# Four of the seven w2 blocks as the moving operand, three as stationary ones, and c and x loaded on the weights' queue, in a one-token transformer block

## The chip, the cores and the metric

The kernel runs on one core of a Trainium2 chip. Times are device microseconds (us) of one execution; where several executions are quoted, it is their median. The profile is one execution taken by the hardware profiler; its span (first to last instruction) is about 1.8 us shorter than the time of the same execution. The runs were made in several sets, each with its own executions of the kernel before ("the same rounds") and not all on one chip: the medians of the kernel before in these sets lie between 427.35 and 427.75 us, so a difference of some 0.2 us is safe only within a set. A ratio of two kernels is the mean time of one's fast runs over the mean of the other's fast runs of the same rounds, so it is not quite the ratio of the medians quoted beside it. The brackets after it are a 95% interval.

## The reference, cut to what matters

Two tokens (one for each of two batch entries) go through one conditioned transformer block. Attention reads a cache of 2 x 4 heads x 32768 x 128 for keys and as much for values, in bf16, 134 MB in all. Then comes an MLP whose second weight, w2, has 3584 x 1024 elements:

```python
mod = (_silu(c) @ w_mod).reshape(c.shape[0], 6, 1, -1)      # c: (2, 1024), w_mod: (1024, 6144)
sa, ca, ga, sb, cb, gb = ...                                # the six slices of mod
h = _layernorm(x) * (1 + ca) + sa
x = x + ga * attention(h, k_cache, v_cache, wq, wo)
h = _layernorm(x) * (1 + cb) + sb
x = x + gb * (gelu(_layernorm(h) @ w1 + b1) @ w2 + b2)      # w2: (3584, 1024)
```

With two tokens, each weight element is used twice. The kernel is a way of reading 178 MB.

## The kernel before: the parts that matter here

All large loads (weights, keys, values, weights) go through one queue, issued by SyncE ("SP") into a ring of buffers. c and x, 4 KB each, are issued by ScalarE ("ACT") at the start:

```python
T.dma("act", lambda e: e.dma_start(c16[:, :], c.rearrange("b (k p) -> (b k) p", p=128)), ...)
T.dma("act", lambda e: e.dma_start(x16[:, :], A_x.rearrange("b o (k p) -> (b o k) p", p=128)), ...)
...   # transposes of c and x, silu, layernorm; then wmod block by block
```

w2 comes in seven blocks q of 512 rows: three loads of two blocks (2 MB each), then block 6 in two pieces, 768 KB (j = 0, 1, 2) and 256 KB (j = 3). There are two ways to multiply a block with gT, the activations (128 rows, 2 useful columns):

- w2 as the *moving* operand: gT is the weight in the array, w2 streams through, 512 columns an instruction. The result is a row in `psS[0]`, spread over four groups of 32 partitions. It has to be copied to SBUF and turned into columns by fp32 matmuls (`to_columns`) before the rest can use it.
- w2 as the *stationary* operand: 128 x 128 pieces of w2 are loaded into the array and only 2 columns of gT move. The result is in columns (`psO`) at once.

```python
for q in range(6):                                   # blocks 0 to 5: w2 moves
    it = need("w2", q // 2)                          # queues the load if it is not yet; what reads it waits
    for j in range(4):
        for hf in range(2):
            t = 2 * (j % 2) + hf
            pe(... matmul(psS[0][32*t:32*t+32, :], lhsT=gT[:, 4*q+j, :], rhs=w[:, q % 2, j*DM+hf*512:j*DM+(hf+1)*512], ...))
load_row("dve", psS[0], "psS0", 3)                   # copy of the row to SBUF
for j in range(4):                                   # block 6: w2 is stationary
    it = need("w2", 3 if j < 3 else 4)
    if j == 3:
        to_columns(psO, "psO", 3, False, False)      # fp32 transposes of the row, added into psO
    for k in range(KT8):
        pe(... matmul(psO[:, 2*k:2*k+2], lhsT=w[:, lo:lo+128], rhs=gT[:, 24+j, 0:2], ...))
dve(mT = psO * mod(5)); dve(res_bf = mT + x1b)
pe(matmul(psM[0:16, 0:128], lhsT=res_bf, rhs=ident)); dve(res16 = psM)   # then the store
```

(The last two lines are in shorthand. `to_columns` has four fp32 matmuls; the profile records each of them twice, so they stand as x8 below.)

## Time and profile before

| | before |
|---|---|
| time, median of 4 runs | 427.35 us (427.31 to 427.46) |
| span of the profiled run | 425.5 us |
| load queue, share of the 16 DMA engines' span | 98.3% |
| third pair of w2 blocks / 768 KB piece / 256 KB piece landed at | 417.73 / 419.57 / 420.21 us |
| first vector step behind w2 (mT) | 422.59 us |

The first fence holds lines of the page of the kernel before: busy time by engine, the slices of the DMA engines (each digit a fortieth of the span, 9 meaning 90% or more) with what they moved, the load queue's line (packets, MB, share of the 16 engines' span), and the chain of waits by engine.

```profile
PE 301.5 (71%) x5116; PEld 236.0 (55%) x5116; DVE 166.9 (39%) x347; ACT 156.8 (37%) x269; POOL 4.9 (1%) x23
...
DMA  8999999999999999999999999999999999999992
GB/s 325 426 430 424 430 436 424 434 424 434 428 436 427 436 427 434 428 436 427 435 428 434 426 436 427 436 427 435 427 434 427 434 429 434 427 430 422 425 429 113
...
q1 hardware_dynamic: 14286, 178.28, 98.3%
...
DMA 79%; PE 18%; ACT 1%; SPq 1%; issue 0%; DVE 0%; DVEq 0%
```

The DMA engines are full from the second slice to the last but one. Most other work fits under them. A change can then pay only before the first byte or behind the last ones. So the tail is what to read. The next fence is the timeline of the kernel before from the second pair of w2 blocks on (start, duration, engine, source line, operation, shapes, and in brackets the engine's idle time and what ended it). L708 are the moving matmuls, L650 is the row copy, L654 are the transposes of the row, L719 the stationary matmuls, L722 is mT.

```profile
412.07 0.63 PE L708 MATMUL psS<-w,gT 128*32 128x512 bf16 x1
...
412.88 1.90 PE L708 MATMUL psS<-w,gT 128*32 128x512 bf16 x16 [0.18 <-DMA w<-in_B_w_dram]
...
417.77 1.90 PE L708 MATMUL psS<-w,gT 128*32 128x512 bf16 x16 [2.99 <-DMA w<-in_B_w_dram]
...
419.62 0.80 PE L719 MATMUL psO<-gT,w 128*128 128x2 bf16 x24
419.72 0.69 DVE L650 COPY S_sb<-psS 128x512 f32<-128x512 f32 x1 [9.06 <-PE psS L708]
...
420.47 1.87 PE L654 MATMUL psO<-half,S_sb 128*128 128x4 f32 x8
...
422.20 0.35 PE L719 MATMUL psO<-gT,w 128*128 128x2 bf16 x8
422.59 0.17 DVE L722 TENSOR_TENSOR mT<-psO,modT 128x16 f32<-128x16 f32 x1 [2.17 <-PE psO L719]
```

The third fence is the end of the chain of waits of the kernel before, followed back from the last instruction (start, us, what).

```profile
387.77 29.96 DMA w<-in_B_w_dram
...
417.77 1.93 PE psS L708 x15
...
419.72 0.70 DVE S_sb L650
...
420.47 1.87 PE psO L654 x8
422.34 0.23 PE psO L719 x8
...
422.59 0.19 DVE mT L722
```

After 414.78 (412.88 + 1.90) PE has nothing to do for 3 us. Then the load lands, and the row copy (0.70) and the transposes (1.87) come behind the last moving matmuls. All loads are in at 420.21, yet mT starts at 422.59, 2.38 us later.

The start, before: x is used at 7.08, the first wmod matmul runs at 10.25, and from the third block on PE waits for the load.

```profile
7.08 0.19 PE L403 MATMUL psM<-ident,x 16*128 16x16 bf16 x1 [2.16 <-DMA x<-in_A_x_dram]
...
10.25 1.04 PE L451 MATMUL psS<-wmod,inT 128*32 128x512 bf16 x8
...
14.85 0.61 PE L451 MATMUL psS<-wmod,inT 128*32 128x512 bf16 x8 [1.85 <-DMA wmod<-in_w_mod_dram]
```

### The profile page before, as it was taken

The numbers are of one execution on the slowest core, as the hardware profiler recorded it, in microseconds if no ns is written. First come the engines' busy times: TensorE is split into PE (matmuls) and PEld (weight loads), VectorE is DVE, ScalarE is ACT, GpSimd is POOL, SyncE is SP. The second block draws the span as 40 slices with busy tenths as digits, with TensorE's granted clock in tenths as the row PEclk, the third lists the DMA queues.
The fourth block names the chain that finished last, engine by engine and source line by source line (L and its number), as shares of the span: only waits on it lengthen the run. The fifth ranks groups of instructions, "written<-read, shape, count | busy, mean of one in ns | idle before, by whom it ended". The sixth has DMA issues, their size and how long they took to land.

```text
span 425.5 us, 11554 instructions
## 1 busy us (share of the span) xinstructions
PE 301.5 (71%) x5116; PEld 236.0 (55%) x5116; DVE 166.9 (39%) x347; ACT 156.8 (37%) x269; POOL 4.9 (1%) x23
## 2 busy tenths in 40 slices
PE   1446478778999789687778958796886773554674
PEld 1105158765877678577567838685774761113243
DVE  1102036544585375256435614662473351101211
ACT  2000026447457348244634724382355335000010
POOL 3000000000000000000000000000000000000000
PEclk9755569968899889698988978898898695655575
DMA  8999999999999999999999999999999999999992
GB/s 325 426 430 424 430 436 424 434 424 434 428 436 427 436 427 434 428 436 427 435 428 434 426 436 427 436 427 435 427 434 427 434 429 434 427 430 422 425 429 113
DMA packets 14367, 178.50 MB, mean 419 GB/s; under 512 B 1543, under 2 KB 1550, under 8 KB 2830
## 3 DMA queue, kind: packets, MB, share of 16 engines
q1 hardware_dynamic: 14286, 178.28, 98.3%
q8 instruction: 9, 0.15, 0.1%
q14 instruction: 8, 0.07, 0.0%
q10 hardware_dynamic: 64, 0.01, 0.0%
HBM read 178.28 MB, written 0.00 MB: 419 GB/s over the span
## 4 chain that ended last, share of the span: by engine, by line
DMA 79%; PE 18%; ACT 1%; SPq 1%; issue 0%; DVE 0%; DVEq 0%
DMA K<-in_A_k_cache_dram 59%; PE psKT L500 11%; DMA wo<-in_A_wo_dram 8%; DMA w<-in_B_w_dram 7%; DMA wmod<-in_w_mod_dram 5%; PE psS L512 3%; PE psO L542 1%; SPq L377 1%; ACT KT_sb L504 1%; PE psS L708 0%; PE psS L641 0%; PE psO L654 0%; ACT E_sb L533 0%; DVE S_sb L650 0%; PE psM L523 0%
## 5 line engine op out<-in xcount | busy, mean ns | idle before, releaser
L500 PE MATMUL psKT<-ident,K 128*128 128x128 bf16 x2048 | 173.4, 236 | 36.8 <-DMA K<-in_A_k_cache_dram 34.4
L500 PEld LDWEIGHTS psKT<-ident,K 128*128 128x128 bf16 x2048 | 132.6, 106 | 48.7 <-DMA K<-in_A_k_cache_dram 42.0
L506 DVE COPY KT_sb<-psKT 128x1024 bf16<-128x1024 bf16 x160 | 108.4, 689 | 116.1 <-PE psKT L500 115.8
L504 ACT ACTIVATE KT_sb<-psKT 128x1024 bf16<-128x1024 bf16 x96 | 98.0, 1021 | 130.5 <-PE psKT L500 130.2
L512 PE MATMUL psS<-qcur,KT_sb 128*128 128x8 bf16 x2048 | 88.3, 168 | 8.3 <-ACT KT_sb L504 7.2
L512 PEld LDWEIGHTS psS<-qcur,KT_sb 128*128 128x128 bf16 x2048 | 79.4, 99 | 13.8 <-ACT KT_sb L504 8.7
L542 PE MATMUL psO<-V,E_sb 128*32 128x512 bf16 x512 | 39.0, 435 | 5.3 <-DMA V<-in_A_v_cache_dram 4.6
L533 ACT ACTIVATE E_sb<-S_sb,negm 128x256 bf16<-128x256 f32 x64 | 32.3, 505 | 9.5 <-DVE negm L529 8.6
L517 DVE TENSOR_REDUCE m1c<-S_sb 128x8 f32<-128x512 f32 x32 | 21.9, 686 | 14.3 <-ACT S_sb L516 13.3
L516 ACT ACTIVATE S_sb<-psS 128x512 f32<-128x512 f32 x32 | 19.0, 592 | 13.9 <-PE psS L512 13.9
L542 PEld LDWEIGHTS psO<-V,E_sb 128*32 128x32 bf16 x512 | 12.0, 104 | 17.5 <-DMA V<-in_A_v_cache_dram 5.6
L451 PE MATMUL psS<-wmod,inT 128*32 128x512 bf16 x64 | 8.0, 593 | 13.4 <-DMA wmod<-in_w_mod_dram 13.4
L641 PE MATMUL psS<-wo,atT 128*32 128x512 bf16 x64 | 7.6, 627 | 12.0 <-DMA wo<-in_A_wo_dram 12.0
L422 ACT ACTIVATE stat<-stat 128x2 f32<-128x2 f32 x3 | 0.6, 203 | 38.4 <-DVE stat L421 38.4
L472 PE MATMUL psS<-wq,inT 128*32 128x512 bf16 x64 | 7.5, 627 | 7.0 <-DMA wq<-in_A_wq_dram 6.0
L533 ACT ACTIVATION_READ_ACCUMULATOR E_sb<-S_sb,negm 128x1 f32 x64 | 12.2, 190 | 0.0
L451 PEld LDWEIGHTS psS<-wmod,inT 128*32 128x32 bf16 x64 | 1.2, 108 | 19.0 <-DMA wmod<-in_w_mod_dram 18.8
L641 PEld LDWEIGHTS psS<-wo,atT 128*32 128x32 bf16 x64 | 1.8, 128 | 16.7 <-DMA wo<-in_A_wo_dram 14.6
L650 DVE COPY S_sb<-psS 128x512 f32<-128x512 f32 x2 | 1.4, 692 | 22.1 <-PE psS L641 13.0
L563 PE MATMUL psM<-msum,hmat 128*128 128x128 f32 x16 | 4.2, 346 | 7.5 <-DVE msum L557 7.5
L457 ACT ACTIVATE S_sb<-psS 128x512 f32<-128x512 f32 x1 | 0.6, 597 | 23.7 <-DVE S_sb L459 23.7
L459 DVE COPY S_sb<-psS 128x512 f32<-128x512 f32 x1 | 0.7, 692 | 21.5 <-PE psS L451 21.5
(115 smaller groups left out, 135.6 us busy)
## 6 DMA issues: line engine op xcount, KB each, us to landing
K<-in_A_k_cache_dram SPq DMA_DIRECT2D x32, 2048.0 KB, 31.7
V<-in_A_v_cache_dram SPq DMA_DIRECT2D x32, 2048.0 KB, 35.0
wmod<-in_w_mod_dram SPq DMA_DIRECT2D x8, 1536.0 KB, 17.8
wq<-in_A_wq_dram SPq DMA_DIRECT2D x4, 2048.0 KB, 37.5
wo<-in_A_wo_dram SPq DMA_DIRECT2D x4, 2048.0 KB, 29.0
w<-in_B_w_dram SPq DMA_DIRECT2D x4, 1792.0 KB, 39.3
w<-in_B_w_dram SPq DMA_DIRECT2D x3, 2048.0 KB, 31.0
w<-in_B_w_dram SPq DMA_DIRECT2D x1, 768.0 KB, 27.8
```

The lines of the kernel that those rows point to most:

```text
L377: T.dma("sp", lambda e, dst=dst, src=cur.src: e.dma_start(dst, src), key=cur.sem, writes=[cur.reg], frees=old)
L451: pe(lambda e, w=it.view, k=k, ch=ch, n=n, q=q: e.matmul(bank[n][32 * q:32 * q + 32, :], lhsT=inT[:, k, :], rhs=w[:, ch * 512:(ch + 1) * 512],
L472: pe(lambda e, w=it.view, k=k, ch=ch, n=n, q=q: e.matmul(bank[n][32 * q:32 * q + 32, :], lhsT=inT[:, k, :], rhs=w[:, k % 2, ch * 512:(ch + ...
L500: pe(lambda e, kq=kq, jj=jj, w=it.view, t=t: e.transpose(psKT[kq][:, jj * 128:(jj + 1) * 128], w[:, t, :], ident[:, :]), reads=[it.reg, "i ...
L504: act(lambda e, src=src: e.activation(KT_sb[g8][:, :, :], src, ACT.Copy), reads=[f"psKT{kq}"], writes=[f"KT_sb{g8}"], sem=f"ev{cc}_{g8}")
L506: dve(lambda e, src=src: e.tensor_copy(KT_sb[g8][:, :, :], src), reads=[f"psKT{kq}"], writes=[f"KT_sb{g8}"], sem=f"ev{cc}_{g8}")
L512: pe(lambda e, t=t, jj=jj: e.matmul(ps[:, t * HPG:(t + 1) * HPG], lhsT=KT_sb[g8][:, jj, :], rhs=qcur[:, :], start=True, stop=True), reads= ...
L516: act(lambda e: e.activation(Sc, ps[:, :].rearrange("p (t h) -> p h t", h=HPG), ACT.Copy), reads=[preg], writes=[f"S_sb{i % 2}_{cc}"], sem ...
L517: dve(lambda e: e.tensor_reduce(m1c[:, :, cc], Sc, AX.X, ALU.max), reads=[f"S_sb{i % 2}_{cc}"], writes=[f"m1c{cc}"])
L533: act(lambda e: e.activation(E_sb[:, :, h, :], S_sb[j][:, h, :].rearrange("p (u t) -> p u t", t=4), ACT.Exp, bias=negm[:, h:h + 1], scale= ...
L542: pe(lambda e, t4=t4, tg=tg, q=q: e.matmul(psO[32 * q:32 * q + 32, :], lhsT=E_sb[:, tg // 4, :, :].rearrange("p h t -> p (h t)"), rhs=it.v ...
L641: pe(lambda e, w=it.view, g=g, j=j, hf=hf, q=q: e.matmul(psS[0][32 * q:32 * q + 32, :], lhsT=atT[g][:, j, :], rhs=w[:, j, hf * 512:(hf + 1 ...
```

## The change

Two edits in one. First, c and x are issued by SyncE behind the first wmod block, on the queue of the weights. Second, only blocks 0 to 3 of w2 stay moving. The row copy and the transposes follow them at once, and blocks 4, 5 and 6 are stationary. The intent is to do the row's detour while PE waits for the third pair, so that only short work stands behind the last landings.

```diff
-    T.dma("act", ... c16 ...)
-    T.dma("act", ... x16 ...)
+    need("wmod", 0)
+    T.dma("sp", ... c16 ...)
+    T.dma("sp", ... x16 ...)
...
-    for q in range(6):
+    for q in range(4):
         it = need("w2", q // 2)
         ...                                    # moving matmuls, as before
     load_row("dve", psS[0], "psS0", 3)
-    for j in range(4):
-        it = need("w2", 3 if j < 3 else 4)
-        if j == 3:
-            to_columns(psO, "psO", 3, False, False)
-        for k in range(KT8):
-            lo = (j if j < 3 else 0) * DM + k * 128
-            pe(... lhsT=w[:, lo:lo + 128], rhs=gT[:, 24 + j, 0:2], start=(j == 0 and k == 0) ...)
+    to_columns(psO, "psO", 3, True, False)
+    for q in range(4, 7):
+        for j in range(4):
+            it = need("w2", 2 if q < 6 else 3 if j < 3 else 4)
+            w = it.view.rearrange("p a n -> p (a n)") if q < 6 else it.view
+            for k in range(KT8):
+                lo = ((q - 4) * 4 + j if q < 6 else j if j < 3 else 0) * DM + k * 128
+                pe(... lhsT=w[:, lo:lo + 128], rhs=gT[:, 4 * q + j, 0:2], start=False ...)
```

(In `to_columns` the start flag is now set on the first of the four matmuls only, since they are the first to write the accumulator.) On PE, 16 moving matmuls go and 64 stationary ones come. Every matmul also has a weight load, so its program grows by 96 instructions. The order of the others doesn't change, apart from the place of the transposes.

More of the change, by code (lines that the diff above doesn't have):

```diff
@@ L389, in pe @@
         T.inst("pe", fn, reads=reads, writes=writes, mark=mark)
-    T.dma("act", lambda e: e.dma_start(c16[:, :], c.rearrange("b (k p) -> (b k) p", p=128)), key="ld_c", writes=["c16"])
-    T.dma("act", lambda e: e.dma_start(x16[:, :], A_x.rearrange("b o (k p) -> (b o k) p", p=128)), key="ld_x", writes=["x16"])
+    need("wmod", 0)
+    T.dma("sp", lambda e: e.dma_start(c16[:, :], c.rearrange("b (k p) -> (b k) p", p=128)), key="ld_c", writes=["c16"])
+    T.dma("sp", lambda e: e.dma_start(x16[:, :], A_x.rearrange("b o (k p) -> (b o k) p", p=128)), key="ld_x", writes=["x16"])
     for t, nm in ((ident, "ident"), (identf, "identf")):
@@ L654, in to_columns @@
             pe(lambda e, i=i: e.matmul(dst[:, 2 * i:2 * i + 16].rearrange("p (h r) -> p h r", r=8)[:, :, 0:2], lhsT=row[:, n * 512 + i * 128:n * 512 + (i + 1) * 128],
-                                       rhs=half[:, :, :], start=start, stop=True, skip_group_check=True),
+                                       rhs=half[:, :, :], start=(start and i == 0), stop=True, skip_group_check=True),
                reads=[f"row{n}", "half"] + ROW, writes=[d_reg], mark=(mark and i == 3))
@@ L709, in bass_adaLN_cond__gqa_block_cached__mixer_channel_mlp__decode_kernel @@
                                                                        rhs=w[:, q % 2, j * DM + hf * 512:j * DM + (hf + 1) * 512],
-                                                                       start=(q == 0 and j < 2), stop=(q == 5 and j >= 2), skip_group_check=True),
+                                                                       start=(q == 0 and j < 2), stop=(q == 3 and j >= 2), skip_group_check=True),
                    reads=[it.reg, "gT"], writes=["psS0"], mark=(j == 3 and hf == 1))
     load_row("dve", psS[0], "psS0", 3)
-    for j in range(4):
-        it = need("w2", 3 if j < 3 else 4)
-        if j == 3:
-            to_columns(psO, "psO", 3, False, False)
-        for k in range(KT8):
-            lo = (j if j < 3 else 0) * DM + k * 128
-            pe(lambda e, w=it.view, j=j, k=k, lo=lo: e.matmul(psO[:, 2 * k:2 * k + 2], lhsT=w[:, lo:lo + 128], rhs=gT[:, 24 + j, 0:2],
-                                                              start=(j == 0 and k == 0), stop=(j == 3), skip_group_check=True),
-               reads=[it.reg, "gT"], writes=["psO"], mark=(j == 3 and k == KT8 - 1))
+    to_columns(psO, "psO", 3, True, False)
[5 more added lines that the diff above has]
+                lo = ((q - 4) * 4 + j if q < 6 else j if j < 3 else 0) * DM + k * 128
+                pe(lambda e, w=w, q=q, j=j, k=k, lo=lo: e.matmul(psO[:, 2 * k:2 * k + 2], lhsT=w[:, lo:lo + 128], rhs=gT[:, 4 * q + j, 0:2],
+                                                                 start=False, stop=(q == 6 and j == 3), skip_group_check=True),
+                   reads=[it.reg, "gT"], writes=["psO"], mark=(q > 4 and j in (2, 3) and k == KT8 - 1))
     dve(lambda e: e.tensor_tensor(mT[:, :, :], psO[:, 0:16].rearrange("p (k b) -> p k b", b=2), mod(5), ALU.mult), reads=["psO", "modT"], writes=["mT"])
```

## The prediction

> **What bounds the kernel.** The input stream. The slice table shows the DMA engines at 90% or more in nearly every slice, about 430 GB/s, until about 416 us of the 425.5 us span; the queue table gives the load queue 98.3% of the engines' span. The chain of waits is 79% DMA. Matmul, vector and scalar work (71%, 39%, 37% busy) hides under it. So time can be won only before the first packet and after the last weights: the tail.
>
> **The tail before (timeline, chain of waits, landings in the trace).** The third pair of w2 blocks lands at 417.73, the next piece (768 KB) at 419.57, the last (256 KB) at 420.21. From there: 16 wide matmuls (128x512 moving, clock 0.5) 417.77 to 419.70; copy of the accumulator row 0.70; fp32 transpose back to columns 1.87 (420.47 to 422.34); 8 stationary matmuls 0.23; then mT at 422.59, two more vector steps, a matmul, the store. The loads are done at 420.21, so about 2.1 us of the chain is row work that no load needs.
>
> **What changes.** Only the first four blocks stay moving; their matmuls end at 414.78, where PE idles 3 us for the load. Row copy (0.70) and transpose (1.87) move into that gap: 414.80 to about 417.45, 0.3 us before the load lands, so they cost nothing. Blocks 4 and 5 cost 64 stationary matmuls in place of 16 wide ones. The 24 stationary ones of before took 0.80 us in all, one starting every 27 ns at clock 0.5 (the last adds its latency). Estimate from that: 64 x 27 ns = 1.7 us, 417.77 to about 419.5, against 1.90. This agrees with the Trainium skill, "TensorE: Matmul & The Clock Gate", section "Back-to-back issue gap": small matmuls have an issue floor near 25 ns. Then 24 behind the 419.57 landing (to 420.25), 8 behind the 420.21 landing: the last starts near 420.45 and mT near 420.65 instead of 422.59. Saving 1.9 us, all on the critical path. After it the tail hangs on the last landing.
>
> **The loads of c and x.** The Trainium skill, "DMA: Bandwidth & Descriptors", section "Issuing engines are not separate DMA queues", says queues of different issuers interleave on the same 16 engines. So moving two 4 KB loads frees no bandwidth. The trace agrees: x, although tiny, lands at 7.03, near the first weight block (7.47). On the one queue c and x should land together at about 7.2 to 7.8; the SP issue of the second block slips 0.9 us (1.18 to about 2.05), long before the first block's 3.7 us of transfer ends. The first weight matmul slips from 10.25 to about 10.8; the PE still waits for the load from the third block on (14.8), so nothing reaches the end. Worth -0.2 to +0.1 us.
>
> **Sum.** 427.33 - 1.9 - 0.1 = 425.3 us, about 0.5% faster. Range 424.5 to 426.4.
>
> **What would show it.** Row copy at about 414.8 and transposes ended before the third pair lands; 64+24+8 stationary matmuls with no gap but the landings; last piece landing still 420.2 +-0.5; mT 0.45 us after it; middle of the kernel unchanged.
>
> **What would make it wrong.** The landing spread over the 16 engines at the end is 3.6 us and one engine is 1.1 us behind the next; it grows where 16 KB instruction fetches (about 1 us each) occupy an engine. The PE's program is 96 instructions longer, and a fetch that stood at 421.4 should now come near 419, while weights still load: on the last engine it would cost up to 1 us. The moved queue entries can also shift which engine is last. Or PE weight loads of 64 blocks run slower than 27 ns (a fetch stall), or the transposes overrun the gap.
>
> Chances: faster by over 2%: 0.005; within 2%: 0.985; slower: 0.01.

## The result, and the profile after

| | before | after |
|---|---|---|
| time, median of 4 runs each | 427.35 us (427.31 to 427.46) | 425.42 us (425.39 to 425.48) |
| ratio after over before | | 0.9955 (0.9937 to 0.9972) |
| span of the profiled run | 425.5 us | 423.6 us |
| third pair / 768 KB / 256 KB landed at | 417.73 / 419.57 / 420.21 | 417.75 / 419.59 / 420.23 us |
| mT starts | 422.59 us | 420.69 us |

The change is 1.93 us, or half a per cent, faster. Every one of the 4 runs after is below every run before. The lines of the page of the changed kernel that answer to those shown of before:

```profile
PE 305.5 (72%) x5164; PEld 244.0 (58%) x5164; DVE 167.3 (39%) x347; ACT 157.1 (37%) x269; POOL 4.9 (1%) x23
...
DMA  8999999999999999999999999999999999999994
GB/s 325 428 430 426 433 434 429 419 432 431 430 436 427 435 425 434 430 432 433 428 435 425 434 432 430 435 427 436 425 432 431 432 433 427 432 430 422 427 428 185
...
q1 hardware_dynamic: 14350, 178.29, 98.7%
...
DMA 76%; PE 16%; SPq 5%; ACT 1%; issue 1%; DVE 0%; ACTq 0%; DVEq 0%
```

The stream is what it was: the slices are full, and the landings in the table agree within 0.02 us. The load queue's share rose to 98.7% because the span behind it got shorter. The timeline of the changed kernel, same stretch (its lines are numbered one or two higher: L709 moving, L651 row copy, L655 transposes, L721 stationary, L724 mT):

```profile
411.54 3.31 PE L709 MATMUL psS<-w,gT 128*32 128x512 bf16 x32 [1.43 <-DVE gT L702]
...
414.90 0.69 DVE L651 COPY S_sb<-psS 128x512 f32<-128x512 f32 x1 [3.51 <-PE psS L709]
...
415.65 1.05 PE L655 MATMUL psO<-half,S_sb 128*128 128x4 f32 x8 [0.80 <-DVE S_sb L651]
...
417.79 2.86 PE L721 MATMUL psO<-gT,w 128*128 128x2 bf16 x96 [1.09 <-DMA w<-in_B_w_dram]
420.69 0.17 DVE L724 TENSOR_TENSOR mT<-psO,modT 128x16 f32<-128x16 f32 x1 [5.09 <-PE psO L721]
```

And the end of its chain of waits:

```profile
386.99 30.76 DMA w<-in_B_w_dram
...
417.79 2.87 PE psO L721 x96
...
420.69 0.19 DVE mT L724
```

The row copy and the transposes stand at 414.90 to 416.70, in the gap. From the landing of the third pair the chain is one group of 96 stationary matmuls, 2.86 us, and then mT. Of the 2.38 us between the last landing and mT, 0.46 is left. The start of the changed kernel:

```profile
7.69 0.19 PE L404 MATMUL psM<-ident,x 16*128 16x16 bf16 x1
...
10.87 1.04 PE L452 MATMUL psS<-wmod,inT 128*32 128x512 bf16 x8
...
14.72 1.04 PE L452 MATMUL psS<-wmod,inT 128*32 128x512 bf16 x8 [1.09 <-DMA wmod<-in_w_mod_dram]
```

c and x land at 7.47 and 7.65 (before: 4.68 and 7.03). PE starts on wmod 0.62 us later, and it waits again for the third block at 14.72 as before. The delay is gone within two blocks.

### The profile page after: what moved, and what is told of

It reads as the page before. It is cut to its first block, busy times and chain, and to the rows that moved or that the text cites. A ratio compares the mean times of both kernels' runs of the same rounds, so it can differ in the third digit from the quotient of the medians.

```text
span 423.6 us, 11650 instructions
## 1 busy us (share of the span) xinstructions
PE 305.5 (72%) x5164; PEld 244.0 (58%) x5164; DVE 167.3 (39%) x347; ACT 157.1 (37%) x269; POOL 4.9 (1%) x23
## 3 DMA queue, kind: packets, MB, share of 16 engines
q1 hardware_dynamic: 14350, 178.29, 98.7%
## 4 chain that ended last, share of the span: by engine, by line
DMA 76%; PE 16%; SPq 5%; ACT 1%; issue 1%; DVE 0%; ACTq 0%; DVEq 0%
DMA K<-in_A_k_cache_dram 60%; PE psKT L501 11%; DMA wo<-in_A_wo_dram 8%; DMA w<-in_B_w_dram 7%; SPq L377 5%; PE psS L513 3%; PE psO L543 1%; PE psO L721 1%; ACT KT_sb L505 1%; ACT E_sb L534 0%; PE psS L642 0%; ACT L534 0%; DVE KT_sb L507 0%; PE psM L524 0%; SPq L392 0%
## 5 line engine op out<-in xcount | busy, mean ns | idle before, releaser
L501 PE MATMUL psKT<-ident,K 128*128 128x128 bf16 x2048 | 180.5, 242 | 36.8 <-DMA K<-in_A_k_cache_dram 34.4
L501 PEld LDWEIGHTS psKT<-ident,K 128*128 128x128 bf16 x2048 | 138.8, 109 | 47.9 <-DMA K<-in_A_k_cache_dram 41.1
L513 PEld LDWEIGHTS psS<-qcur,KT_sb 128*128 128x128 bf16 x2048 | 80.7, 100 | 13.1 <-ACT KT_sb L505 8.4
L543 PE MATMUL psO<-V,E_sb 128*32 128x512 bf16 x512 | 35.6, 406 | 1.9 <-DMA V<-in_A_v_cache_dram 1.0
L460 DVE COPY S_sb<-psS 128x512 f32<-128x512 f32 x1 | 0.7, 691 | 20.7 <-PE psS L452 20.7
L558 DVE SCALAR_TENSOR_TENSOR msum<-psO,mk,msum 128x128 f32<-128x128 f32 x24 | 8.4, 351 | 0.9
```

The lines of the kernel that those rows point to most:

```text
L501: pe(lambda e, kq=kq, jj=jj, w=it.view, t=t: e.transpose(psKT[kq][:, jj * 128:(jj + 1) * 128], w[:, t, :], ident[:, :]), reads=[it.reg, "i ...
L513: pe(lambda e, t=t, jj=jj: e.matmul(ps[:, t * HPG:(t + 1) * HPG], lhsT=KT_sb[g8][:, jj, :], rhs=qcur[:, :], start=True, stop=True), reads= ...
L543: pe(lambda e, t4=t4, tg=tg, q=q: e.matmul(psO[32 * q:32 * q + 32, :], lhsT=E_sb[:, tg // 4, :, :].rearrange("p h t -> p (h t)"), rhs=it.v ...
L558: dve(lambda e, q=q: e.scalar_tensor_tensor(out=msum[:, :], in0=psO[:, q * 128:(q + 1) * 128], scalar=mk4[:, q:q + 1], in1=msum[:, :], op0 ...
```

## The experiments

**Which half pays?** Two runs, each with one half of the diff. The edit of the first is the first six lines of the diff above alone, the edit of the second is all the rest alone.

> Only the first half of the change: c and x on the weights' queue behind the first block, w2 as before. My theory (the gain is row work taken out of the tail): same time as before, 427.3 us, within 0.2; c and x land near 7.5 and 7.7, first weight matmul near 10.9 instead of 10.25, last weight piece still near 420.2, mT still 2.4 us after it. Rival (moving the small loads made the stream start or end earlier and is part of the 1.9 us): 426.9 or less, with the last piece landing earlier.

Measured: 427.78 us (427.11 to 428.69, 4 runs; before in the same rounds 427.55, 427.11 to 427.66), ratio 1.0008 (0.9989 to 1.0026). Its spans were 425.3 to 425.6 us, those of before in the same rounds too, so the scatter of the times lies outside the span. In its trace c and x land at 7.32 and 7.49, the last piece at 420.11, and mT starts 2.37 us after it. What follows: no change that these runs could see, as the theory has it.

> Only the second half: w2 as in the change, c and x on the other queue as before. My theory: 425.4 us, within 0.2, as fast as the whole change; x lands near 7.0 again; mT 0.45 us after the last landing. Rival (the small loads carry part of it): 425.9 or more.

Measured: 425.47 us (425.35 to 425.55), ratio 0.9953 (0.9937 to 0.9970). Last landing 420.22, mT at 420.68. What follows: the w2 half is the whole gain.

**The place of the transposes, or the cheaper matmuls?** The stationary blocks of the change are kept, but the transposes go back to where they were:

```diff
-    to_columns(psO, "psO", 3, True, False)
     for q in range(4, 7):
         for j in range(4):
             ...
+            if (q, j) == (6, 3):
+                to_columns(psO, "psO", 3, False, False)
             for k in range(KT8):
-                ... start=False ...
+                ... start=(q == 4 and j == 0 and k == 0) ...
```

> As the change (four moving, three stationary blocks), but the eight fp32 transposes of the row stay where they were before, between the last 24 and the last 8 stationary matmuls. My theory (what paid is the place of the transposes, not the cheaper matmuls): the transposes start near 420.3, take 1.9 us at clock 0.5 (1.05 at clock 1.0), then 0.4 for the last 8: 427.1 us at clock 0.5, 426.3 at clock 1.0. Rival (the gain is that 64 narrow matmuls replace 16 wide ones): 425.4.

Measured: 427.08 us (426.95 to 427.22), ratio 0.9992 (0.9975 to 1.0009). The timeline of this run shows the transposes (L655) at clock 0.5 between the last landing (420.15) and mT (L725):

```profile
417.70 2.65 PE L722 MATMUL psO<-gT,w 128*128 128x2 bf16 x88 [2.93 <-DMA w<-in_B_w_dram]
...
420.22 1.85 PE L655 MATMUL psO<-half,S_sb 128*128 128x4 f32 x8
...
421.92 0.35 PE L722 MATMUL psO<-gT,w 128*128 128x2 bf16 x8
422.31 0.17 DVE L725 TENSOR_TENSOR mT<-psO,modT 128x16 f32<-128x16 f32 x1 [6.80 <-PE psO L722]
```

What follows: with the same stationary blocks and the transposes late, 1.66 of the 1.93 us are lost again (427.08 - 425.42, by the medians; 1.61 against the w2 half alone, in the same rounds). The place pays. Of the gain 0.22 us is left by the trace (mT comes 2.16 us after the last landing, before it was 2.38). It belongs to the cheaper matmuls and to the row copy, which no longer stands behind the third pair; no run separates these two.

**Do the first blocks have to move?** All seven blocks stationary, with no row, no copy and no transposes:

```diff
-    for q in range(4):
-        ...                        # moving matmuls
-    load_row("dve", psS[0], "psS0", 3)
-    to_columns(psO, "psO", 3, True, False)
-    for q in range(4, 7):
+    for q in range(7):
         for j in range(4):
-            it = need("w2", 2 if q < 6 else ...)
+            it = need("w2", q // 2 if q < 6 else ...)
             ...                    # offset and start flag to match
```

> All seven blocks of w2 stationary: no moving blocks, no row, no transposes; 128 more narrow matmuls near 411.5 to 415, before the third pair lands. My theory (after the change only the last landing and the 8 matmuls behind it count, and the first four blocks have slack either way): 425.4 us, within 0.2, mT 0.45 us after the last landing. Rival (the first blocks had to be moving for the PE to keep up with the loads): the third pair's matmuls start after its landing plus more than 0.1 us, and the time is over 425.8.

Measured: 425.66 us (425.57 to 425.82), ratio 0.9959 (0.9942 to 0.9976); 0.26 us above the 425.4 expected, and 0.19 above the w2 half alone in the same rounds. The timeline of this run:

```profile
411.56 3.55 PE L710 MATMUL psO<-gT,w 128*128 128x2 bf16 x128 [1.43 <-DVE gT L702]
...
417.74 1.87 PE L710 MATMUL psO<-gT,w 128*128 128x2 bf16 x64 [2.63 <-DMA w<-in_B_w_dram]
...
419.86 1.01 PE L710 MATMUL psO<-gT,w 128*128 128x2 bf16 x32 [0.26 <-DMA w<-in_B_w_dram]
420.91 0.18 DVE L713 TENSOR_TENSOR mT<-psO,modT 128x16 f32<-128x16 f32 x1 [9.50 <-PE psO L710]
```

PE does keep up. It is done with the first four blocks at 415.11, the third pair starts within 0.05 us of its landing (417.69), and mT stands 0.48 us after the last landing, as in the change. But the landings behind the third pair are 0.2 us late: 419.81 and 420.43. Neither theory had that. The trace has one record for each DMA packet and for each engine's share of a landing. From these I worked out the list below: by how much each of the three last of the 16 engines is behind the first one, for the last loads. Above it stand the 16 KB instruction fetches of one queue (q8; start in us, duration in ns) from 380 us on. I take it for the queue that feeds PE: the fetch that stood at 421.41 before came at 419.86 with 96 more instructions on PE.

```
                  change                        all stationary
fetches           402.213 (924) 419.861 (959)   401.810 (961) 416.602 (961) 420.940 (1348)
third pair        2.08  2.30  3.54              2.24  2.25  3.47
768 KB piece      2.06  2.27  3.53              2.23  3.45  3.73
256 KB piece      2.02  2.25  3.52              2.19  3.45  3.70
```

The trace does not name the engines, so they are told apart by these lags alone. One engine carries the end in the change: it is more than 1.2 us behind all others, and so it is in the all-stationary kernel up to the third pair. In the all-stationary kernel the next fetch came at 416.60 instead of 419.86, before the loads were done, and a second engine fell back by about 1.2 us or more. One of the two is now the last, 0.2 us later than before. That was a guess as to cause, so it was tested.

**An instruction fetch as the cause.** The change, plus 88 unused transposes to move the fetch without touching the tail (after the w1 matmuls of k = 1):

```diff
+            for m in range(88):
+                pe(... transpose(psKT[0][:, (m % 8)*128:(m % 8 + 1)*128], ident, ident) ...)
```

> The change plus 88 unused 128x128 transposes on the PE near 391 us, where it waits for loads. They make the PE's program as long as the all-stationary one without touching the tail. My theory (the all-stationary run was 0.2 us slower because a 16 KB instruction fetch moved from 419.9 to 416.6, where it took about 1 us of an engine that was still loading): the ninth fetch of that queue comes before 418, a second engine joins the last one at a lag of over 3.4 us, the last piece lands near 420.4, and the time is 425.6. Rival (128 more narrow matmuls in the tail were themselves the cost): last landing 420.2, 425.4.

Measured: 429.27 us (428.12 to 430.19), ratio 1.0033 (1.0011 to 1.0054). A miss of mine. PE does not wait for loads there: it comes out of the layernorms at about 398 with landed w1 blocks before it and is busy without a break. The windows of this run (stretch, its length, then busy us and number of instructions of PE, PE weight loads, DVE, ACT and POOL, then granted clock, DMA share and GB/s):

```profile
398.00:402.00 4.00, 3.92 (x34) 2.62 (x35) 0.00 (x0) 0.00 (x0) 0.00 (x0) 0.50 1.01 428
402.00:406.00 4.00, 4.00 (x59) 4.00 (x57) 0.00 (x0) 0.00 (x0) 0.00 (x0) 0.76 1.01 421
```

The dummies stood on the critical path of PE, and the first w2 matmul came at 416.44 instead of 411.54. That shows something else: the slack of PE ahead of the tail is small. In the change PE waits only 1.1 us (416.70 to 417.79) for the third pair, so 4.9 us more work could not fit. The landings themselves answered the question by half. The fetch came at 414.70, the second engine went from 2.39 (at the second pair) to 3.65 (at the third) behind the first, but not past the last one (3.72), and the last piece landed at 420.19.

The clean form puts matmuls of two columns where PE really waits, between the four blocks of wo:

```diff
     # after the matmuls of wo block g
+        for m in range((44, 22, 22, 0)[g]):
+            pe(... matmul(psM[:, 400:402], lhsT=ident, rhs=ident[:, 0:2]) ...)
```

> The clean form of the dummy run, whose 88 wide transposes made the PE late: the change plus 88 unused matmuls of two columns (27 ns each), placed between the four blocks of wo, where the PE waits for loads anyway. My theory (an instruction fetch that comes before its engine has finished pushes that engine back by over 1 us): the ninth 16 KB fetch comes before 418, the second-slowest engine goes from a lag of about 2.3 us to 3.4 or more, the matmuls of w2 start where they did in the change (11 us before the end), and the last piece lands at 420.2 to 420.45 depending on which of the two engines is then last: 425.4 to 425.65 us. Rival (the second late engine in the all-stationary run came from 128 more weight loads in the tail, not from the fetch): the second engine stays near 2.3 and the time is 425.4.

Measured: 425.40 us (425.19 to 425.55), ratio 0.9951 (0.9936 to 0.9967). The same list for this run:

```
                  change + 88 short matmuls
fetches           386.344 (967) 414.753 (967) 420.551 (946)
second pair       1.87  1.88  3.40
third pair        1.91  3.36  3.39
256 KB piece      1.90  3.31  3.38
```

What follows: with a fetch at 414.75, a second engine fell back by about 1.5 us (from 1.88 at most to 3.36), with no work added to the tail. That is the mechanism seen in the all-stationary run, shown without its 128 extra matmuls. Whether the last landing moves depends on where that engine stood before: here it stopped just short of the last engine, and the time is that of the change. The sizes fit afterwards: with a shift of 1.48 the second engine of the all-stationary run, at 2.25, comes to 3.73, as its list shows, and passes the last one (3.47) by about 0.26. With the shift of the dummies run (1.26 at least) it could have been as little as 0.04. So the mechanism is shown, and the 0.2 us is put down to it by the trace of that one run and this estimate.

The traces also tell where the lag of the last engine came from, which was not asked. In all 14 of them it grows in two steps: in the change from 2.01 to 2.76 us at the load that lands at 244, and from 2.54 to 3.60 at the one that lands at 323. After that it stays to the end. Beside both steps stands an 8 KB fetch of the other instruction queue (q14), at 239.74 and at 319.59. No run moved these fetches, so this is a coincidence in time, seen 14 times, and not a test.

**What sets the end after the change?** The last block in one load of 1 MB instead of 768 + 256 KB:

```diff
-    add(("w2", 3), [3 * DM], w2_v[:, 6, 0:3 * DM], 144 * KB)
-    add(("w2", 4), [DM], w2_v[:, 6, 3 * DM:4 * DM], 150 * KB)
+    add(("w2", 3), [4 * DM], w2_v[:, 6, 0:4 * DM], 144 * KB)
     ...                            # and the matmuls wait for this one
```

> The change, but the last block of w2 comes as one load of 1 MB, so 32 stationary matmuls instead of 8 stand behind the last landing. My theory (after the change the end is the last landing plus the matmuls behind it, 27 ns each, plus a fixed rest): last landing unchanged near 420.2, mT 24 x 27 ns = 0.64 us later, 426.05 us. Rival (the PE's own work of 96 weight loads sets the end): 425.4.

Measured: 426.00 us (425.92 to 426.04), ratio 0.9964 (0.9949 to 0.9979). Last landing 420.12, then 32 matmuls, mT at 421.22, 1.10 us behind instead of 0.46: 0.64 us more, as expected. The other way, with only 64 KB (2 matmuls) in the last load:

```diff
+    add(("w2", 3), [4 * DM - 256], w2_v[:, 6, 0:4 * DM - 256], 144 * KB)
+    add(("w2", 4), [256], w2_v[:, 6, 4 * DM - 256:4 * DM], 152 * KB - 512)
     ...                            # and each matmul waits for the load that holds its columns
```

> The change, but only 64 KB (2 matmuls) is left for the last load instead of 256 KB (8 matmuls). My theory: 6 x 27 ns = 0.16 us less behind the last landing, unless the earlier piece, now landing within 0.2 us of the last, keeps the PE busy past it (30 matmuls, 0.80 us, from about 420.05): then mT stays within 0.1 of the change, and the time is 425.3 to 425.5. Rival of a landing-only end: 425.25.

Measured: 425.79 us (425.69 to 426.13), ratio 0.9959 (0.9945 to 0.9972): slower than the change. The expectation was wrong in its own arithmetic. Its last lines named the 30 matmuls that now hang on the 960 KB piece (0.80 us, by 27 ns each), but they were booked as costing 0.1. The timeline of this run:

```profile
417.97 1.87 PE L723 MATMUL psO<-gT,w 128*128 128x2 bf16 x64 [1.10 <-DMA w<-in_B_w_dram]
...
420.26 1.01 PE L723 MATMUL psO<-gT,w 128*128 128x2 bf16 x32 [0.42 <-DMA w<-in_B_w_dram]
421.31 0.17 DVE L726 TENSOR_TENSOR mT<-psO,modT 128x16 f32<-128x16 f32 x1 [5.55 <-PE psO L723]
```

The pieces landed at 420.21 and 420.40. 32 matmuls begin at 420.26 and mT comes at 421.31, 0.91 us behind the last landing. This profile is of the slowest of the five executions (426.13 us). In it the third pair at 417.92 and the last piece at 420.40 are both 0.17 later than in the change, and the tail is 0.45 longer. The four others have spans of 423.9 to 424.0 us, against its 424.2, and were not profiled; so this trace shows where the loss lies, and not how much of it the median holds. The split of before was a good one. Between the landings of the two pieces of the change lie 0.64 us for 8 matmuls, that is 80 ns of landing a matmul against 27 ns of PE time. With n matmuls in the last piece, the first piece lands 80n ns before the last landing, and PE then needs (32 - n) x 27 ns for it. PE is done with the first piece just as the last one lands at about n = 8: an estimate from these two numbers, and the kernels' own value.

**A version that beats both.** First the addend alone, beside the small last piece: x1b (residual plus bias) is put into the output accumulator by an fp32 matmul in the wait before the third pair, and the vector step that added it later goes.

```diff
+    pe(... matmul(psM[0:16, 0:128], lhsT=x1b, rhs=identf, start=True) ...)      # before to_columns
-    dve(mT = psO * mod(5)); dve(res_bf = mT + x1b)
-    pe(matmul(psM[0:16, 0:128], lhsT=res_bf, rhs=ident, start=True))
+    dve(res_bf = psO * mod(5))
+    pe(matmul(psM[0:16, 0:128], lhsT=res_bf, rhs=ident, start=False))           # adds to x1b
```

> The change with the small last piece, and the residual plus bias is put into the output accumulator by an fp32 matmul in the wait before the third pair, so that the vector step that added it after the last matmul (0.23 us plus its hand-over) goes. My theory (everything after the last landing is one chain, each step of it counts in full): 0.25 to 0.3 us less than the small-piece run, about 425.1. Rival (the store's completion or something else covers that step): no difference from the small-piece run.

Measured: 425.62 us (425.50 to 425.71), ratio 0.9956 (0.9942 to 0.9970), against 425.79 of the small-piece run in the same rounds. From the last landing to the final matmul it took 1.19 us (420.19 to 421.38) against 1.40 (420.40 to 421.80). So 0.21 us less, the length of the mT step with its hand-over, not the 0.25 to 0.3 expected; the sum 425.1 carried over the small-piece error. Then the last block in three loads, so that PE can work off each while the next lands:

```diff
+    CUT = (0, 22 * 128, 30 * 128, 32 * 128)
+    for n in range(3):
+        add(("w2", 3 + n), [CUT[n + 1] - CUT[n]], w2_v[:, 6, CUT[n]:CUT[n + 1]], 144 * KB + 2 * CUT[n])
     ...                            # in place of the two loads of block 6; the addend first, as above
```

> A version meant to beat both: the change, with residual plus bias put into the output accumulator beforehand (one vector step of 0.21 us less behind the last matmul), and the last block of w2 in three loads (22, 8 and 2 matmuls) so that the PE is not left with 30 matmuls behind a late piece as in the small-piece run. My theory: the PE runs 96 matmuls without a gap of more than 0.15 us from the third pair's landing, the last ends 0.3 us after the last landing, and the time is 425.1 us, 0.3 less than the change. Rival (more, smaller loads slow the end of the stream): last landing later than 420.3, 425.3 or more.

Measured: 425.08 us (424.93 to 425.26, 5 runs), ratio 0.9943 (0.9930 to 0.9957). Its timeline, where the step behind the 96 matmuls is already the last vector step before the final matmul:

```profile
417.68 2.79 PE L727 MATMUL psO<-gT,w 128*128 128x2 bf16 x96 [0.88 <-DMA w<-in_B_w_dram]
420.50 0.23 DVE L730 TENSOR_TENSOR res_bf<-psO,modT 128x16 bf16<-128x16 f32 x1 [4.82 <-PE psO L727]
```

The landings are 417.63, 419.32, 419.99 and 420.18; the vector step starts 0.32 us behind the last (mT of the change: 0.46). So by the traces about 0.14 us of its gain come from the three loads, and 0.21 from the vector step that is gone; no run has the addend with the old split. To compare with the change itself, both ran once more, on one chip and in the same rounds:

> The change as it is, once more, so that it shares chip and rounds with the three-piece version: 425.4 us, mT 0.46 us after the last landing as in its first profile.

> The three-piece version again, on the same chip and in the same rounds as the change. My theory: 0.3 to 0.4 us less than the change (the last small matmul starts 0.60 us after the last landing instead of 0.95), about 425.1. Rival (the 0.3 us between the two came from different chips): within 0.1 us of the change.

Measured: the change 425.36 us (425.30 to 425.57, 6 runs; ratio to before 0.9940, 0.9926 to 0.9954), the three-piece version 425.15 us (425.03 to 425.22, 6 runs; ratio 0.9933, 0.9919 to 0.9948). Every run of it is below every run of the change: 0.21 us by the medians, less than the 0.3 to 0.4 expected, and more than the 0.1 of the rival (other chips). It beats both kernels, by little. Both give the reference's result, as did all kernels run here.

## Why the prediction was right

- *The time.* 425.3 us was predicted, with 424.5 to 426.4 as the range; 425.42 was measured. The saving was put at 1.9 for the tail and 0.1 for the start. The tail gave all of the 1.93; the run with the loads alone shows nothing at the start, though its noise (ratio 0.9989 to 1.0026) could hide 0.1 us. The trace agrees: mT moved from 422.59 to 420.69, by 1.90 us.
- *What bounds the kernel.* Right: the last landing stayed within 0.02 us, and the chain before it is loads. All other slack (3 us of PE before the third pair) was there to be used.
- *The row's detour costs nothing in the gap.* Right, and the late-transposes run shows that this is the step that pays. The size was off: the transposes were put at 1.87 us and took 1.05 in the profiled run after, because the granted clock was 1.0 there and not 0.5. In the run with the w2 half alone they took 1.87 us in the same place, and the time was the same. Off the chain, the clock did not matter here.
- *64 stationary matmuls in 1.7 us.* Right: the 768 KB piece's matmuls begin at 419.63, directly behind its landing at 419.59, so the 64 were done by then; by the trace's records one starts every 27 ns. The Trainium skill, "TensorE: Matmul & The Clock Gate", section "Back-to-back issue gap", gives an issue floor of about 25 ns for small matmuls at full clock. The stationary matmuls of w2 start 27 ns apart at clock 0.5, and those of the attention scores, with weight loads of the same size, 25 ns apart at clock 1.0 (medians over the trace of before).
- *mT 0.45 us behind the last landing.* Right: 0.46 was measured.
- *c and x.* Predicted to land at 7.2 to 7.8: 7.47 and 7.65. First weight matmul predicted at 10.8: 10.87. The Trainium skill, "DMA: Bandwidth & Descriptors", section "Issuing engines are not separate DMA queues", says that queues of different issuers run on the same engines and only save issue time; the two-halves runs (427.78 and 425.47 us against 427.55 and 425.42) show no gain from one queue instead of two.
- *The instruction fetch.* Named as the main risk, expected "near 419": it came at 419.86, when all but the last engine had landed their share of the last piece (by 418.96), and the last landing did not move. The prediction had no reason why the fetch should miss the one engine that was still loading: that part was luck. Its "up to 1 us" was also too small for what a fetch can do to an engine (1.26 to 1.48 us in the runs with dummies). The all-stationary run shows how close it was.

## What to carry to other kernels

Where loads bound a kernel, look for what stands between the last landing and the store, and ask of each step whether it needs the last bytes. Work that needs only earlier data (a copy, a transposition of layout, an addend) belongs into the wait before the last load, even if the matmuls that this leaves for the last data are more in number. Cut the last load so that the matmuls of one piece are done when the next lands; too small a last piece only moves the pile to the piece before it.

## What the Trainium skill lacked or had wrong

- "Runtime: NRT & Kernel Launch", section "Instruction fetch mechanics", says that instructions are fetched in 16 KiB blocks on a DMA queue of the sequencer's own and that the cost is mostly hidden. The trace agrees on the 16384 bytes, 0.92 to 0.97 us for seven of the eight fetches listed above, and no gap of PE at the fetch of 419.86 is seen in the tail of the change. The page does not say what a fetch costs the loads: one engine's landings fell back by about 1.5 us in the run with short dummies (from 1.88 at most to 3.36 us behind the first engine), and in the all-stationary run the end of the stream came 0.2 us later.
- "DMA: Bandwidth & Descriptors": no figure of how unequal the 16 engines of one load can be, beyond a table row that has two of them as usually slower. Here the last engine's share of each load landed 3.4 to 3.7 us behind the first one's at the end of all runs, and mostly more than 1.1 us behind the next to last. The end of the kernel hangs on it.
- "TensorE: Matmul & The Clock Gate", section "Weight-path perf modes — Fast Weight Load (FWL) and DoubleRow", gives about 2x as measured for the fast weight load. At clock 0.5 the pairs of a 128x128 bf16 weight load and a matmul of 2 columns started 27 ns apart, against 107 ns by the same page, section "LDWEIGHTS (loading the stationary operand)", for a plain load (128 columns over 1.2 GHz): an estimate of 4x from that figure, so more than the page's measured one. The trace shows the pace alone: the record of one such weight load is 104 ns long and overlaps the next ones, so that the fast load is what gives the pace is not shown.
